# Reordering the first loads, centring before the first transposes, moving two transposes to DMA, and splitting the last output tile of a fused attention + gMLP kernel

## The chip, the cores and the metric

The kernel runs on one core of a Trainium2 chip. The metric is device time in microseconds (us) of one execution; lower is better. All executions told of here were fast (granted TensorE clock 0.994 to 1.0). A "profile" or "trace" is one execution recorded by the hardware profiler; its span is about 1.7 us shorter than the time of the same execution.

Engines: PE is TensorE (matmuls), PEld its weight loads, DVE is VectorE, ACT is ScalarE, POOL is GpSimd, SP is SyncE, which only issues DMAs here. A "q" after an engine's name (SPq) means its sequencer.

## The reference, cut to what matters

With S = 2048 tokens, D = 512, 32 heads of 16, a sliding window of 256, and Fh = 688:

```python
xn = layernorm(x)                                   # over D
A  = attention(xn @ wqkv) @ wo                      # causal, window 256
z  = gelu(xn @ w_in)                                # (S, 1376)
z1, z2 = z[:, :688], layernorm(z[:, 688:])
g  = w_sp @ z2 + b_sp[:, None]                      # mixes over tokens
out = x + A + (z1 * g) @ w_out
```

## The kernel before

Tokens are cut into 16 tiles of 128. The program has three stages. First, for each tile: normalise x on VectorE, transpose it (so that D lies on the partitions), and compute z in two halves of 688 columns on TensorE; q, k and v units for blocks of 512 tokens are put between the halves from tile 3 on. Then the last nine q, k, v units and the first scores: the hand-over. Then scores, exponentials, the token mixing g and the output tiles f, interleaved by a list made at build time. These are the parts that the change touches:

```python
# loads, in the order of issue (nc.sync = SyncE, nc.scalar = ScalarE)
load_x(nc.sync, 0, 1)
load_x(nc.scalar, 1, 2)
load_x(nc.sync, 2, 3)
load_x(nc.scalar, 3, 4)
nc.sync.dma_start(out=w_in_sb[:, :, 0:FH], in_=w_in_v[:, :, 0:FH])     # first half of w_in
nc.sync.dma_start(out=w_in_sb[:, :, FH:F], in_=w_in_v[:, :, FH:F])     # second half
load_x(nc.sync, 4, 8)
nc.sync.dma_start(out=wqkv[:], in_=A_wqkv.rearrange("(c p) f -> p c f", p=P))
# ... the rest of x, b_sp, wo, w_out; zero fill of v_bd on POOL, DVE and ACT;
#     13 warm-up matmuls on zeros ...

def ln_apply(n):            # xn = (x - mean) * rstd; rstd is a power taken on GpSimd
    ...
def transposes(n, xn):
    if n >= 8:
        nc.sync.dma_start_transpose(out=xnT[:, :, n * P : (n + 1) * P], in_=xn[:])
        return
    tp = psum["f"].tile([P, NC, P], BF, name="tp", tag="f")
    for c in range(NC):
        nc.tensor.transpose(out=tp[:, c, :], in_=xn[:, c * P : (c + 1) * P], identity=ident[:])
    nc.scalar.copy(out=xnT[:, :, n * P : (n + 1) * P], in_=tp[:])

def z_half(n, half):        # 8 matmuls of 344 columns, then gelu on ScalarE
    zp = ps_s.tile([P, 2, 512], F32, name="zp", tag="S")
    for c in range(NC):
        for j in range(2):
            f0 = half * FH + j * HALF
            nc.tensor.matmul(zp[:, j, 0:HALF], lhsT=xnT[:, c, n * P : (n + 1) * P],
                             rhs=w_in_sb[:, c, f0 : f0 + HALF], ...)
    nc.scalar.activation(out=..., in_=zp[:, :, 0:HALF], func=ACT.Gelu_apprx_tanh)

# start of the main loop over tiles, cut: z_half(0,0), transposes(1), z_half(0,1),
# transposes(2), z_half(1,0), z_half(1,1), transposes(3), ...

# in f_work(t), the output tile: ten matmuls of 512 columns, one addition, one store
nc.vector.tensor_tensor(out=xo[:], in0=fo[:], in1=xo[:], op=ALU.add)
eng.dma_start(out=out2[t * P : (t + 1) * P, :], in_=xo[:])
```

The softmax here doesn't subtract the row's maximum and nothing guards it: scores larger than these inputs give would overflow.

Of the kernel before, what the change touches and what calls it, by code (L numbers as in the profile page):

```python
# [8 lines left out]
P = 128  # L9
# [6 lines left out]
D = 512  # L16
# [21 lines left out]
OBUF = 8  # L38
UBUF = 4

@with_exitstack
def kernel(
# [50 lines left out]
    def qkv_unit(b, i):  # L93
# [22 lines left out]
        else:  # L116
# [11 lines left out]
            for e in range(2):  # L128
                for kk in range(2):
                    nc.sync.dma_start(  # L130
                        out=v_bd[e * KB : (e + 1) * KB, v_at(2 * n + kk, e), :, :],
                        in_=st[kk * KB : (kk + 1) * KB, e, :, :],
                    )
# [9 lines left out]

    qkv_list = [(b, i) for b in range(4) for i in (0, 1, 8, 2, 3, 9, 4, 5, 10, 11, 6, 7)]

# [8 lines left out]
    with ExitStack() as actx:  # L154
# [11 lines left out]

        w_in_v = B_w_in.rearrange("(c p) f -> p c f", p=P)
        load_x(nc.sync, 0, 1)
        load_x(nc.scalar, 1, 2)
        load_x(nc.sync, 2, 3)  # L170
        load_x(nc.scalar, 3, 4)
        nc.sync.dma_start(out=w_in_sb[:, :, 0:FH], in_=w_in_v[:, :, 0:FH])
        nc.sync.dma_start(out=w_in_sb[:, :, FH:F], in_=w_in_v[:, :, FH:F])
        load_x(nc.sync, 4, 8)
        nc.sync.dma_start(out=wqkv[:], in_=A_wqkv.rearrange("(c p) f -> p c f", p=P))
        load_x(nc.sync, 8, 12)
        load_x(nc.sync, 12, 16)
        with nc.allow_non_contiguous_dma(reason="tiny bias gather"):
            nc.sync.dma_start(out=b_bf[:], in_=B_b_sp.rearrange("(n p) -> p n", p=P))
        nc.sync.dma_start(out=wo_sb[:], in_=A_wo.rearrange("(c p) n -> p c n", p=P))  # L180
        nc.sync.dma_start(
            out=w_out_sb[:, 0:5, :], in_=B_w_out[0:640, :].rearrange("(c p) n -> p c n", p=P)
        )
        nc.vector.memset(w_out_sb[:, 5, :], 0.0)
        nc.sync.dma_start(out=w_out_sb[0:48, 5, :], in_=B_w_out[640:688, :])

# [3 lines left out]
        nc.vector.memset(warm[:], 0.0)  # L190
        wz = lt.tile([P, P], BF, name="wz", bufs=1)
        nc.vector.memset(wz[:], 0.0)
        nc.gpsimd.memset(v_f[:, 0:2560], 0.0)
        nc.vector.memset(v_f[:, 2560:4608], 0.0)
        wps = psum["o"].tile([P, 512], F32, name="wps", tag="o")
        for _ in range(13):
            nc.tensor.matmul(
                wps[:], lhsT=wz[:], rhs=wz[:].unsqueeze(1).to_broadcast([P, 4, P]),
                start=True, stop=True,
            )  # L200
        nc.scalar.activation(out=warm[:, 0:4], in_=warm[:, 4:8], func=ACT.Gelu_apprx_tanh)
        zsrc = warm[:, 4:5].to_broadcast([P, VZ - 4608])
        nc.scalar.copy(out=v_f[:, 4608:VZ], in_=zsrc)
        make_identity(nc, ident[:])
        def setup_early():
            nc.vector.reduce_sum(
                out=hmask[:],
                in_=ident[:].rearrange("p (s e d) -> p e s d", s=4, e=2),
                axis=mybir.AxisListType.XY,
            )  # L210
            for e in range(2):
                nc.vector.memset(v_bd[e * KB : (e + 1) * KB, NKB, :, e : e + 1], 1.0)

        def setup_late():
# [36 lines left out]
        def ln_batch(b0, k):  # L251
            mvt = sm.tile([P, 4, 2], F32, name="mvt")
            for n in range(b0, b0 + k):
# [5 lines left out]
                yield  # L259

        def ln_apply(n):
            xs = xts[n // 4][:, n % 4, :]
            xn = lt.tile([P, D], BF, name="xn")
            nc.vector.tensor_scalar(
                out=xn[:], in0=xs, scalar1=mvx[n], scalar2=rsx[n],
                op0=ALU.subtract, op1=ALU.mult,
            )
            return xn

        def transposes(n, xn):  # L270
            if n >= 8:
                nc.sync.dma_start_transpose(out=xnT[:, :, n * P : (n + 1) * P], in_=xn[:])
                return
            tp = psum["f"].tile([P, NC, P], BF, name="tp", tag="f")
            for c in range(NC):
                nc.tensor.transpose(  # L276
                    out=tp[:, c, :], in_=xn[:, c * P : (c + 1) * P], identity=ident[:]
                )
            nc.scalar.copy(out=xnT[:, :, n * P : (n + 1) * P], in_=tp[:])

        def z_half(n, half):
            zp = ps_s.tile([P, 2, 512], F32, name="zp", tag="S")
            for c in range(NC):
                for j in range(2):
                    f0 = half * FH + j * HALF
                    nc.tensor.matmul(  # L286
                        zp[:, j, 0:HALF],
                        lhsT=xnT[:, c, n * P : (n + 1) * P],
                        rhs=w_in_sb[:, c, f0 : f0 + HALF],
                        start=(c == 0), stop=(c == NC - 1),  # L290
                    )
            dst = (z1 if half == 0 else z2n)[:, n, :]
            nc.scalar.activation(  # L293
                out=dst.rearrange("p (j f) -> p j f", j=2),
                in_=zp[:, :, 0:HALF], func=ACT.Gelu_apprx_tanh,
            )

# [21 lines left out]
        xns = {}  # L319
        for _ in ln_batch(0, 1):  # L320
            pass
        for _ in ln_batch(1, 1):
            pass
        xns[0] = ln_apply(0)
        for _ in ln_batch(2, 1):
            pass
        xns[1] = ln_apply(1)
        for _ in ln_batch(3, 1):
            pass
        for n in range(2, 4):  # L330
            xns[n] = ln_apply(n)
        transposes(0, xns.pop(0))

        z_rs = {}
        for n in range(NB):
            b, j = divmod(n, 4)
            z_half(n, 0)
            if n == 0:
                transposes(1, xns.pop(1))
            elif n == 6:  # L340
                setup_late()
            elif n in (9, 10):
                load_wsp(n - 9)
            if b < 3:
                if j < 2:
                    for _ in ln_batch(4 * b + 4 + 2 * j, 2):
                        pass
                if 1 <= j < 3:
                    for m in range(2):
                        k = 4 * b + 4 + 2 * (j - 1) + m  # L350
                        xns[k] = ln_apply(k)
                        if k >= 8:
                            transposes(k, xns.pop(k))
            if n >= 1:
                r = z_stats(n - 1)
                if r is not None:
                    z_rs[n - 1] = r
            if n >= 3:
                for _ in qkv_unit(*qkv_list.pop(0)):
                    pass  # L360
            z_half(n, 1)
            if n == 0:
                transposes(2, xns.pop(2))
            elif n == 1:
                transposes(3, xns.pop(3))
                setup_early()
# [4 lines left out]
            if n >= 3:  # L371
                for _ in range(2):
                    for _ in qkv_unit(*qkv_list.pop(0)):
                        pass
            if b == 0 and j >= 2:
                for m in range(2):
                    k = 4 + 2 * (j - 2) + m
                    transposes(k, xns.pop(k))
        nc.scalar.activation(out=warm[:, 0:4], in_=warm[:, 4:8], func=ACT.Exp)
# [36 lines left out]
    def e_tile(u):  # L416
        i = u % NE
        if i not in E_sb:
            E_sb[i] = Et = (ep if i < 2 else late()).tile([P, EW], BF, name=f"E{i}", bufs=1)
            nc.vector.memset(  # L420
                Et[:, 0 : 8 * (REG + KB)].rearrange("p (r c) -> p r c", c=REG + KB)[:, :, 0:KB],
                0.0,
            )
            nc.vector.memset(Et[:, 4 * ROW : TOFF], 0.0)
        return E_sb[i]

    for u in range(2):
# [61 lines left out]
    def f_work(t):  # L489
# [4 lines left out]
        xo = xos.pop(t)  # L494
        fo = ps_x.tile([P, 512], F32, name="fo", tag="f")
        for ch in range(NFC):
            nc.tensor.matmul(  # L497
                fo[:], lhsT=uTs[t][:, ch, :], rhs=w_out_sb[:, ch, :],
                start=(ch == 0), stop=False,
            )  # L500
            yield 512 / 2400.0
        for c in range(NC):
            nc.tensor.matmul(  # L503
                fo[:], lhsT=oTs[t][:, c, :], rhs=wo_sb[:, c, :],
                start=False, stop=(c == NC - 1),
            )
            yield 512 / 2400.0
        nc.vector.tensor_tensor(out=xo[:], in0=fo[:], in1=xo[:], op=ALU.add)  # L508
        eng = nc.sync if t >= NB - 2 else nc.gpsimd
        eng.dma_start(out=out2[t * P : (t + 1) * P, :], in_=xo[:])  # L510
        yield -on_dve(0.7)
# [113 lines left out]
    def do_mask(u, kind):  # L625
        Et = e_tile(u)
        mAC, mCA = mACA[:, 0:2, :], mACA[:, 1:3, :]
        if kind == "T":
# [120 lines left out]
```

## Time and profile before

Six executions took 273.22 to 275.02 us, median 273.87.

| Reading | Value | View |
|---|---|---|
| TensorE busy | 264.4 of 272.3 us | the page, part 1 |
| waits of TensorE for data | 4.3 us, all before 11 us | the wait table |
| TensorE idle from 18 to 80 us, and from 80 to 268 us | 0 and about 0.2 us | the table of stretches |
| first half of w_in lands, second half lands | 8.36, 10.59 us | the trace |
| last matmul to end of span | 3.4 us | timeline |

The head of the page of the kernel before, with busy time and share of the span for each engine:

```profile
span 272.3 us, 8364 instructions
PE 264.4 (97%) x3565; PEld 160.5 (59%) x3565; DVE 153.8 (56%) x421; ACT 198.3 (73%) x269; POOL 35.7 (13%) x80
```

The wait table of TensorE in the kernel before (total us, times, longest us):

```profile
PE zp L286 <- DMA w_in_sb<-in_B_w_in_dram: 2.7, 2, 2.0
PE wps L197 <- DVE wz L192: 1.4, 1, 1.4
PE tp L276 <- DVE xn L264: 0.2, 1, 0.2
```

Two stretches of the kernel before (stretch, its length, then busy us of PE, PEld, DVE, ACT and POOL with counts, the granted clock, the DMA share and GB/s):

```profile
18.00:80.00 62.00, 62.00 (x361) 34.77 (x360) 41.86 (x123) 38.42 (x60) 10.00 (x20) 1.00 0.38 80
95.00:240.00 145.00, 144.90 (x2847) 94.28 (x2847) 82.31 (x221) 137.06 (x177) 13.85 (x34) 1.00 0.52 96
```

TensorE sets the pace from 11 us to the last matmul. ScalarE is nearly as full from 95 to 240 us (137.06 of 145 us), but nothing shows TensorE waiting for it. So what can be won lies at the two ends. The timeline of TensorE at the start of the kernel before (start us, us, engine, line, operation, output and inputs, shape, count, and in brackets the idle time before it and who ended it):

```profile
6.01 0.40 PE L276 MATMUL tp<-ident,xn 128*128 128x128 bf16 x4 [0.23 <-DVE xn L264]
8.40 1.33 PE L286 MATMUL zp<-w_in_sb,xnT 128*128 128x344 bf16 x8 [2.00 <-DMA w_in_sb<-in_B_w_in_dram]
9.57 0.39 PE L276 MATMUL tp<-ident,xn 128*128 128x128 bf16 x4
10.63 1.33 PE L286 MATMUL zp<-w_in_sb,xnT 128*128 128x344 bf16 x8 [0.68 <-DMA w_in_sb<-in_B_w_in_dram]
11.80 0.39 PE L276 MATMUL tp<-ident,xn 128*128 128x128 bf16 x4
```

After 10.63 us there is no gap. TensorE has then one z half and one transpose group behind it (1.17 + 0.23 us by their starts), so the stream runs as if it had begun at 9.23 us. And the end, the last VectorE addition of the kernel before:

```profile
268.95 0.69 DVE L508 TENSOR_TENSOR xo<-fo,xo 128x512 bf16<-128x512 f32 x1 [1.47 <-PE fo L503]
```

### The profile page before, as it was taken

The numbers are of one execution on the slowest core, as the hardware profiler recorded it, in microseconds if no ns is written. First come the engines' busy times: TensorE is split into PE (matmuls) and PEld (weight loads), VectorE is DVE, ScalarE is ACT, GpSimd is POOL, SyncE is SP. The second block draws the span as 40 slices with busy tenths as digits, with TensorE's granted clock in tenths as the row PEclk, the third lists the DMA queues.
The fourth block names the chain that finished last, engine by engine and source line by source line (L and its number), as shares of the span: only waits on it lengthen the run. The fifth ranks groups of instructions, "written<-read, shape, count | busy, mean of one in ns | idle before, by whom it ended". The sixth has DMA issues, their size and how long they took to land.

```text
span 272.3 us, 8364 instructions
## 1 busy us (share of the span) xinstructions
PE 264.4 (97%) x3565; PEld 160.5 (59%) x3565; DVE 153.8 (56%) x421; ACT 198.3 (73%) x269; POOL 35.7 (13%) x80
## 2 busy tenths in 40 slices
PE   7699999999999999999999999999999999999995
PEld 2465555555554566667675666757575666766652
DVE  7597965954637465645645655565556466522222
ACT  7477556555567889999999999999999999200000
POOL 6122412111101001010101010101010101101110
PEclk9999999999999999999999999999999999999999
DMA  6975141375211248452709273637161446456621
GB/s 208 376 185 181 40 78 39 83 94 120 45 30 24 50 62 171 94 141 42 147 3 173 48 116 74 113 25 162 31 158 37 112 61 128 90 126 144 144 70 59
DMA packets 73078, 27.84 MB, mean 102 GB/s; under 512 B 62944, under 2 KB 71568, under 8 KB 73040
## 3 DMA queue, kind: packets, MB, share of 16 engines
q1 hardware_dynamic: 71312, 23.10, 41.9%
q0 software_dynamic: 1440, 3.93, 4.9%
q8 instruction: 28, 0.46, 0.7%
q10 hardware_dynamic: 288, 0.26, 0.3%
q14 instruction: 10, 0.08, 0.1%
HBM read 8.41 MB, written 2.10 MB: 39 GB/s over the span
## 4 chain that ended last, share of the span: by engine, by line
PE 90%; DMA 4%; DVE 2%; ACT 1%; SPq 1%; issue 0%; POOL 0%; DVEq 0%; ACTq 0%; POOLq 0%
PE gf L469 27%; PE o L540 14%; PE zp L286 13%; PE S L593 9%; PE fo L497 8%; PE fo L503 5%; PE pj_f L100 4%; PE pj_o L100 4%; DMA w_in_sb<-in_B_w_in_dram 3%; PE pj_f L119 2%; PE pj_o L119 2%; ACT E L614 1%; DMA v_bd<-vst 1%; PE tp L276 0%; SPq L130 0%; ACT kst L109 0%
## 5 line engine op out<-in xcount | busy, mean ns | idle before, releaser
L614 ACT ACTIVATE E<-S 128x1024 bf16<-128x1024 f32 (+3 forms) x184 | 141.5, 893 | 1.2 <-DMA v_bd<-vst 0.7
L469 PE MATMUL gf<-z2n,wspT 128*128 128x344 bf16 x512 | 85.0, 310 | 0.0
L469 PEld LDWEIGHTS <-wspT 128*128 128x128 bf16 x512 | 45.9, 97 | 25.5 <-issue 2.6
L620 DVE TENSOR_TENSOR E<-E,mACA 128x1024 bf16<-128x1024 bf16 (+1 forms) x92 | 42.4, 500 | 11.6 <-ACT E L614 11.1
L540 PEld LDWEIGHTS <-E 128*128 128x128 bf16 x1440 | 41.7, 96 | 6.9 <-issue 2.4
L540 PE MATMUL o<-v_bd,E 128*128 128x48 bf16 x1440 | 45.0, 183 | 0.0
L286 PE MATMUL zp<-w_in_sb,xnT 128*128 128x344 bf16 x256 | 42.2, 309 | 2.7 <-DMA w_in_sb<-in_B_w_in_dram 2.7
L475 DVE SCALAR_TENSOR_TENSOR u<-gf,b_all,z 128x344 bf16<-128x344 f32 x32 | 18.4, 575 | 38.3 <-PE gf L469 31.0
L286 PEld LDWEIGHTS <-xnT 128*128 128x128 bf16 x256 | 24.8, 98 | 18.0 <-issue 2.0
L593 PE MATMUL S<-qT,kpad 32*128 32x192 bf16 (+3 forms) x960 | 30.4, 231 | 0.1
L510 POOL DMA_DIRECT2D out_dram<-xo x14 | 7.6, 545 | 146.7 <-DVE xo L508 146.7
L497 PE MATMUL fo<-w_out_sb,uT 128*128 128x512 bf16 x96 | 24.4, 379 | 0.0
L593 PEld LDWEIGHTS <-kpad 32*128 32x128 bf16 x960 | 14.0, 92 | 17.5 <-issue 16.6
L508 DVE TENSOR_TENSOR xo<-fo,xo 128x512 bf16<-128x512 f32 x16 | 11.1, 691 | 22.1 <-PE fo L503 22.1
L111 DVE TENSOR_SCALAR kpad<-kst,hmask 128x512 bf16<-128x512 bf16 x32 | 9.8, 349 | 22.1 <-ACT kst L109 22.0
L246 POOL TENSOR_TENSOR rs<-ve,mhalf 128x2 f32<-128x2 f32 (+1 forms) x18 | 12.4, 687 | 66.1 <-DVE ve L243 66.1
L293 ACT ACTIVATE z<-zp 128x688 bf16<-128x688 f32 x16 | 11.9, 743 | 11.8 <-PE zp L286 11.8
L293 ACT ACTIVATE z2n<-zp 128x688 bf16<-128x688 f32 x16 | 11.9, 743 | 11.5 <-PE zp L286 11.5
L100 PEld LDWEIGHTS <-wqkv 128*128 128x128 bf16 x128 | 12.5, 98 | 11.9
L503 PE MATMUL fo<-wo_sb,oT 128*128 128x512 bf16 x64 | 17.3, 380 | 0.0
L100 PE MATMUL pj_o<-xnT,wqkv 128*128 128x512 bf16 x64 | 16.4, 379 | 0.0
L100 PE MATMUL pj_f<-xnT,wqkv 128*128 128x512 bf16 x64 | 16.4, 379 | 0.0
(54 smaller groups left out, 179.7 us busy)
## 6 DMA issues: line engine op xcount, KB each, us to landing
v_bd<-vst SPq DMA_DIRECT2D x64, 32.0 KB, 1.9
xo<-in_A_x_dram POOLq DMA_DIRECT2D x16, 128.0 KB, 3.4
out_dram<-xo POOLq DMA_DIRECT2D x14, 128.0 KB, 2.6
xt<-in_A_x_dram SPq DMA_DIRECT2D x3, 512.0 KB, 11.8
wqkv<-in_A_wqkv_dram SPq DMA_DIRECT2D x1, 1536.0 KB, 12.7
w_in_sb<-in_B_w_in_dram SPq DMA_DIRECT2D x2, 688.0 KB, 7.5
w_out_sb<-in_B_w_out_dram SPq DMA_DIRECT2D x1, 640.0 KB, 5.9
wo_sb<-in_A_wo_dram SPq DMA_DIRECT2D x1, 512.0 KB, 11.7
```

Source lines behind the costliest of these rows:

```text
L100: nc.tensor.matmul(pt[:], lhsT=wqkv[:, c, w0 : w0 + P], rhs=xnT[:, c, t0 : t0 + 512], start=(c == 0), stop=(c == NC - 1),)
L246: nc.gpsimd.tensor_tensor(out=rs[:, 0:k], in0=ve[:, 0:k], in1=mhalf[:, 0:k], op=ALU.pow)
L286: nc.tensor.matmul(zp[:, j, 0:HALF], lhsT=xnT[:, c, n * P : (n + 1) * P], rhs=w_in_sb[:, c, f0 : f0 + HALF], start=(c == 0), stop=(c == NC ...
L293: nc.scalar.activation(out=dst.rearrange("p (j f) -> p j f", j=2), in_=zp[:, :, 0:HALF], func=ACT.Gelu_apprx_tanh,)
L469: nc.tensor.matmul(gf[:, 0:HALF], lhsT=wspT[t][:, c, :], rhs=z2n[:, c, j * HALF : (j + 1) * HALF], start=(c == 0), stop=(c == NB - 1),)
L475: nc.vector.scalar_tensor_tensor(out=u[:, j * HALF : (j + 1) * HALF], in0=gf[:, 0:HALF], scalar=b_all[:, t : t + 1], in1=z1[:, t, j * HALF ...
L497: nc.tensor.matmul(fo[:], lhsT=uTs[t][:, ch, :], rhs=w_out_sb[:, ch, :], start=(ch == 0), stop=False,)
L503: nc.tensor.matmul(fo[:], lhsT=oTs[t][:, c, :], rhs=wo_sb[:, c, :], start=False, stop=(c == NC - 1),)
L540: nc.tensor.matmul(o[:, q, s, :], lhsT=Et[:, col : col + P], rhs=v_bd[:, v_at(kb, 0) : v_at(kb, 1) + 1 : kb + 1, 4 * G + s, :], start=(i = ...
L593: nc.tensor.matmul(S[s // 2][:, s % 2, col : col + n * KB], lhsT=kpad[32 * s : 32 * s + 32, G, kb, :, :].rearrange("p e k -> p (e k)"), rh ...
L614: nc.scalar.activation(out=dst, in_=src, func=ACT.Exp, scale=SM_SCALE)
L620: nc.vector.tensor_tensor(out=ap, in0=ap, in1=m.unsqueeze(1).to_broadcast([P, ap.shape[1], 2, KB]), op=ALU.mult,)
```

## The change

The intent is to give TensorE useful work earlier, take a little work off it, and shorten the end. In short:

1. Loads: x blocks 2 and 3 go behind the first half of w_in; its second half comes as two quarters; all from SyncE; the later loads are held back.
2. Tiles 0 and 1 are centred (mean subtracted) and transposed at once on TensorE; 1/std goes into the scale of the gelu. For q, k and v they are also normalised and transposed by DMA.
3. The z half (0,1) is done in two quarters, with tile 1's first half between them.
4. Tiles 6 and 7 are transposed by DMA, not on TensorE.
5. Hand-over: another order of the last q, k, v units, half of the last v transfers from GpSimd, gap memsets of the exponentials' buffers later.
6. The last output tile is done in 320 + 192 columns.
7. Smaller things at the start: the warm-up is cut into 8 + 6 matmuls (13 before), a part of ScalarE's zero fill goes to GpSimd, and the transposed copies of tiles 1 and 2 are made by VectorE.

```diff
         load_x(nc.sync, 0, 1)
-        load_x(nc.scalar, 1, 2)
+        load_x(nc.sync, 1, 2)
+        load_w(0, FH)
         load_x(nc.sync, 2, 3)
-        load_x(nc.scalar, 3, 4)
-        nc.sync.dma_start(out=w_in_sb[:, :, 0:FH], in_=w_in_v[:, :, 0:FH])
-        nc.sync.dma_start(out=w_in_sb[:, :, FH:F], in_=w_in_v[:, :, FH:F])
+        load_w(FH, FH + HALF)
+        load_x(nc.sync, 3, 4)
+        load_w(FH + HALF, F)
         load_x(nc.sync, 4, 8)
-        nc.sync.dma_start(out=wqkv[:], in_=A_wqkv.rearrange("(c p) f -> p c f", p=P))
+        (q and k thirds of wqkv here; v third and x 8..15 in load_more(), after the first tiles;
+         b_sp, wo, w_out in load_late(), at tile 7)
...
-        for _ in range(13):          (warm-up matmuls)
+        warm_up(8)                   (six more after the first transposes)
...
+        def ln_center(n):
+            xc = lt.tile([P, D], BF, name="xn")
+            nc.vector.tensor_scalar(out=xc[:], in0=xts[n // 4][:, n % 4, :], scalar1=mvx[n],
+                                    scalar2=None, op0=ALU.subtract)
+            return xc
-        def transposes(n, xn):
-            if n >= 8:
+        def transposes(n, xn, centered=False):
+            if not centered and (n < 2 or n >= DMA_T):       (DMA_T = 6)
                 nc.sync.dma_start_transpose(out=xnT[:, :, n * P : (n + 1) * P], in_=xn[:])
...
+            if n == 0:
+                xc1 = ln_stats_center(1)
+                ln_only(2)
+                z_half(0, 0)
+                transposes(1, xc1, True)
+                transposes(0, ln_apply(0))
+                xns[2] = ln_apply(2)
+                transposes(1, ln_apply(1))
+                load_more()
+                z_half(0, 1, (0,))
+                continue
             z_half(n, 0)
+            if n == 1:
+                transposes(2, xns.pop(2)); ln_only(3); xns[3] = ln_apply(3)
+                z_half(0, 1, (1,))
...
-        fo = ps_x.tile([P, 512], F32, name="fo", tag="f")       (ten matmuls, addition, store)
+        parts = [(0, D)] if t < NB - 1 else [(0, 320), (320, D)]
+        for a, b in parts:                                      (the same on columns a:b)
```

## The prediction

> **What bounds the kernel now.** TensorE. The page gives it 264.4 us busy of a 272.3 us span; the wait table has only 4.3 us of waits, all before 11 us; in the table of stretches TensorE idles 0.2 us in all between 18 and 268 us. ScalarE is nearly full from 95 to 238 us, but TensorE shows no wait for it. So only an earlier start of useful TensorE work, less of it, or a shorter tail can help. Of 7.9 us idle, some 4.5 are at the start and 3.4 after the last matmul (268.9 us).
>
> **Start.** The chain of waits begins with w_in's transfer: its first half lands at 8.4 us, its second at 10.6; only from 10.63 us does TensorE run without a gap. By then it had done one z half (1.17 us in the chain) and one transpose group (0.23), so the stream behaves as if begun at 9.2 us. The change puts x blocks 2 and 3 (256 KB) behind the first w_in half and splits the second into two quarters with 688-byte rows; z_half(0,1) is split to match. In 0.5 us slices, the DMA engines move 250 to 340 GB/s from 2.5 us on, so 256 KB less in front is about 0.8 us: first half at about 7.6 us. The centred transpose takes the GpSimd power (0.57 us) off the way of x block 0; its xcT should be ready near 6 us, before the weights, so by itself it buys nothing. The next quarter lands at about 9.1 to 9.5 us; TensorE wants it at 9.0. I allow 0.2 to 0.5 us of stalls. The Trainium skill, "DMA: Bandwidth & Descriptors", Specifications, puts the line-rate minimum at 512 B, so 688 B should be no disaster; no run here shows that yet. Net: 1.3 us (0.5 to 1.7).
>
> **Work removed.** Tiles 6 and 7 are transposed by DMA: two groups of about 0.22 us, 0.45 us. Tiles 0 and 1 get both a TensorE transpose (centred) and a DMA transpose for q, k, v. Those queue behind 3.5 MB of loads and are needed near 16.5 us; I expect them at 15 to 16 us. This is the thinnest margin.
>
> **Hand-over (80 to 98 us).** With v transfers earlier and on two queues and gap memsets later, VectorE's 1.8 us wait for v_bd and ScalarE's 0.7 us go away, but TensorE idled only about 0.2 us there. Gain 0.1 us.
>
> **Tail.** The last tile is split 320+192. The last VectorE addition falls from 0.69 to about 0.36 us (estimate by columns plus a fixed part); ten more short matmuls add some 0.05; the last store (1.7 us to landing) is mostly fixed cost. Gain 0.3 us.
>
> **Sum:** 1.3 + 0.45 + 0.1 + 0.3 = 2.1 us of 273.87: predicted 271.7 us, range 270.5 to 273.1. Faster by over 2%: 0.02; within 2%: 0.96; slower by over 2%: 0.02.
>
> **Right or wrong would show as:** first z matmul at about 7.6 us (before: 8.40) and gapless TensorE from about 11.5 us with more work done; 24 transposing matmuls instead of 32; VectorE's wait for v_bd gone while TensorE's idle there hardly changes; the end 3.1 us after the last matmul instead of 3.4.
>
> **What would make it wrong:** quarters moving slower than halves; DMA transposes of tiles 0 and 1 landing after 16.5 us, which stalls the first q unit; TensorE's clock falling back in the new warm-up; ScalarE pacing the middle, so that an earlier start is swallowed there.

## The result, and the profile after

The changed kernel took 270.43 to 270.97 us in eight runs, median 270.82; the kernel before, 273.72 us (median of 16). The ratio is 0.9889, with a 95% interval of 0.9873 to 0.9905. A ratio here is the mean time of one kernel's fast runs over that of the other's in the same rounds, so it is not quite the ratio of the medians. The gain is 2.9 us, 1.1%: inside the range of the prediction, but only 0.3 us from its lower end, and 0.8 us more than forecast. The spread also shrank, from 2.1 us (272.9 to 275.02) to 0.5 us.

The head of the page of the changed kernel, and its wait table of TensorE:

```profile
span 269.0 us, 8406 instructions
PE 264.3 (98%) x3568; PEld 160.7 (60%) x3568; DVE 155.3 (58%) x426; ACT 197.0 (73%) x267; POOL 40.3 (15%) x88
```

```profile
PE wps L204 <- DVE wz L191: 1.1, 1, 1.1
PE zp L342 <- DMA w_in_sb<-in_B_w_in_dram: 0.5, 1, 0.5
PE gf L556 <- DVE on L641: 0.3, 1, 0.3
```

TensorE is busy as long as before; what went is idle time. The wait for w_in fell from 2.7 to 0.5 us; one new wait of 0.3 us appeared in the hand-over. The timeline of TensorE at the start of the changed kernel:

```profile
4.66 0.42 PE L311 MATMUL tp<-ident,xn 128*128 128x128 bf16 x4
4.92 1.46 PE L204 MATMUL wps<-wz 128*128 128x512 bf16 x6
6.91 1.33 PE L342 MATMUL zp<-w_in_sb,xcT 128*128 128x344 bf16 x8 [0.53 <-DMA w_in_sb<-in_B_w_in_dram]
8.07 0.39 PE L311 MATMUL tp<-ident,xn 128*128 128x128 bf16 x4
8.42 0.74 PE L324 MATMUL zo<-w_in_sb,xcT 128*128 128x344 bf16 x4
9.00 1.33 PE L342 MATMUL zp<-w_in_sb,xcT 128*128 128x344 bf16 x8
```

From 6.91 us on it runs almost without a gap: the quarter at 8.42 us costs about 0.1 us. The last additions of the changed kernel, one for each part of the last tile:

```profile
265.40 0.49 DVE L597 TENSOR_TENSOR xo<-fo,xo 128x320 bf16<-128x320 f32 x1 [0.67 <-PE fo L592]
266.22 0.36 DVE L597 TENSOR_TENSOR xo<-fo,xo 128x192 bf16<-128x192 f32 x1 [0.33 <-PE fo L592]
```

To see where the time came from, I read four marks of TensorE's stream in each trace (starts in us; the fourth is the end of the last matmul):

```
               first z   first q,k,v   first score   last matmul ends   span
before           8.40       18.52         89.95          268.91         272.3
after            6.91       15.96         87.22          266.19         269.0
gained           1.49        2.56          2.73            2.72           3.3
```

The lines behind the marks, from the timelines of TensorE, first in the kernel before and then in the changed one (first q, k, v unit, first score, last matmuls):

```profile
18.52 1.03 PE L100 MATMUL pj_o<-xnT,wqkv 128*128 128x512 bf16 x4
89.95 0.37 PE L593 MATMUL S<-qT,kpad 32*128 32x192 bf16 x8
267.88 1.03 PE L503 MATMUL fo<-wo_sb,oT 128*128 128x512 bf16 x4
```

```profile
15.96 1.03 PE L101 MATMUL pj_o<-xnT,wqkv 128*128 128x512 bf16 x4
87.22 0.37 PE L682 MATMUL S<-qT,kpad 32*128 32x192 bf16 x8
265.69 0.49 PE L592 MATMUL fo<-wo_sb,oT 128*128 128x192 bf16 x4
```

(These two profiled executions lie 3.3 us apart; the medians 2.9.) The 2.56 us before the first q, k, v unit hold the 0.45 us of two transpose groups: the kernel before has done tiles 4 and 5 by then, the changed one does them just after, and later has no groups for 6 and 7. So the start gave 2.1 us, the transposes 0.45, the hand-over 0.16, the stage from the first score to the last matmul nothing, and the tail 0.55.

The trace also tells when each of the 16 shares of a DMA (one for each DMA engine) reported its landing. Here for the first half of w_in:

```
                 first   9th      12th   last share      second half, last share
before            5.82    6.55    6.74     8.36               10.59
after             5.68    6.03    6.18     6.87                9.80
```

The fastest share gained 0.14 us and the slowest 1.49. TensorE waits for the slowest. The 9th of the 16 came 0.52 us earlier; the rest of the 1.49 is that the last two shares no longer come 1.6 us behind the 12th. That was not foreseen, and most experiments below ask for its cause.

### The profile page after: what moved, and what is told of

It is laid out like the page before. It is cut to its first block, busy times and chain, and to the rows that moved or that the text cites. A ratio compares the mean times of both kernels' runs of the same rounds, so it can differ in the third digit from the quotient of the medians.

```text
span 269.0 us, 8406 instructions
## 1 busy us (share of the span) xinstructions
PE 264.3 (98%) x3568; PEld 160.7 (60%) x3568; DVE 155.3 (58%) x426; ACT 197.0 (73%) x267; POOL 40.3 (15%) x88
## 4 chain that ended last, share of the span: by engine, by line
PE 96%; DMA 2%; DVE 1%; SPq 0%; issue 0%; DVEq 0%
PE gf L556 29%; PE o L629 14%; PE zp L342 14%; PE S L682 9%; PE fo L586 8%; PE pj_o L101 6%; PE fo L592 5%; PE pj_f L101 5%; PE pj_f L120 3%; PE pj_o L120 2%; DMA w_in_sb<-in_B_w_in_dram 2%; PE zo L324 0%; PE tp L311 0%; SPq L164 0%; DVE u L562 0%
## 5 line engine op out<-in xcount | busy, mean ns | idle before, releaser
L342 PE MATMUL zp<-w_in_sb,xnT 128*128 128x344 bf16 x224 | 37.2, 309 | 0.0
L342 PEld LDWEIGHTS <-xnT 128*128 128x128 bf16 x224 | 21.7, 98 | 14.1 <-ACT xnT L315 0.3
L586 PE MATMUL fo<-w_out_sb,uT 128*128 128x512 bf16 (+2 forms) x102 | 24.5, 367 | 0.0
L597 DVE TENSOR_TENSOR xo<-fo,xo 128x512 bf16<-128x512 f32 (+2 forms) x17 | 11.2, 660 | 21.6 <-PE fo L592 21.6
L101 PE MATMUL pj_o<-xnT,wqkv 128*128 128x512 bf16 x72 | 18.5, 379 | 0.0
L351 ACT ACTIVATE z<-zp 128x688 bf16<-128x688 f32 x14 | 10.4, 743 | 10.2 <-PE zp L342 10.2
L592 PE MATMUL fo<-wo_sb,oT 128*128 128x512 bf16 (+2 forms) x68 | 17.5, 368 | 0.0
L351 ACT ACTIVATE z2n<-zp 128x688 bf16<-128x688 f32 x14 | 10.4, 743 | 9.3 <-PE zp L342 9.3
L641 DVE TENSOR_TENSOR on<-o,rsum 128x128 bf16<-128x128 f32 x64 | 15.6, 286 | 1.4 <-DVE rsum L639 0.3
```

What stands on the lines that cost most here:

```text
L101: nc.tensor.matmul(pt[:], lhsT=wqkv[:, c, w0 : w0 + P], rhs=xnT[:, c, t0 : t0 + 512], start=(c == 0), stop=(c == NC - 1),)
L342: nc.tensor.matmul(zp[:, j, 0:HALF], lhsT=xcT[n][:, c, :] if n in xcT else xnT[:, c, n * P : (n + 1) * P], rhs=w_in_sb[:, c, f0 : f0 + HAL ...
L351: nc.scalar.activation(out=dst.rearrange("p (j f) -> p j f", j=2), in_=zp[:, :, 0:HALF], func=ACT.Gelu_apprx_tanh, scale=rsx[n] if n in xc ...
L586: nc.tensor.matmul(fo[:, a:b], lhsT=uTs[t][:, ch, :], rhs=w_out_sb[:, ch, a:b], start=(ch == 0), stop=False,)
L592: nc.tensor.matmul(fo[:, a:b], lhsT=oTs[t][:, c, :], rhs=wo_sb[:, c, a:b], start=False, stop=(c == NC - 1),)
L641: nc.vector.tensor_tensor(out=o_norm[J][q][:, G * P : (G + 1) * P].rearrange("p (s e d) -> p s e d", e=2, d=DH), in0=o[:, q, :, :].rearran ...
```

## The experiments

Each kernel was run against the kernel before on the same chip. "Changed kernel + edit" starts from the changed one. The intervals on the ratios are 0.2 to 0.4% each way, mostly from the spread of the kernel before; where a few tenths of a microsecond matter I lean on the marks in the traces. "Worse than the changed kernel" compares medians taken in different rounds and on different chips. By the ratios the losses would be 0.6 us (a_xfirst), 0.3 (a_twoqueues), 0.7 (a_zorder), 0.2 (a_handover), 0.4 (a_whole), 2.4 (a_nocentre) and 1.8 (a_t8tail), so a few tenths either way are not settled.

### Which part of the load order brings the weights earlier?

**b_onequeue**: the kernel before, all x loads from SyncE.

```diff
-        load_x(nc.scalar, 1, 2)
+        load_x(nc.sync, 1, 2)
-        load_x(nc.scalar, 3, 4)
+        load_x(nc.sync, 3, 4)
```

> The kernel before, with x blocks 1 and 3 issued from SyncE like the others, same order of loads (x0, x1, x2, x3, first half of w_in). Before: first w_in half landed at 8.36 us, 12 of its 16 engine shares by 6.74, the last two 1.6 us later; after: last at 6.87, 12th at 6.18. Order theory (only the 256 KB in front matter): landing 8.4 us or later, time as before. Queue theory (the second issuing queue leaves a few DMA engines behind): spread between 12th and last share under 0.8 us, landing about 7.6 us, time 0.7 us better. Fill theory (ScalarE's zero fill of v_bd, which ran to 6.4 us before and 4.9 us after, slows the transfer): fill ends about 0.9 us earlier, landing some 0.4 us better.

Measured: 273.40 us, ratio 0.9992 (0.9967 to 1.0018). First half landed at 8.52 us, 12th share at 7.43. The queue theory falls as it was put: nothing came earlier and the time stayed. The test is not clean, though. With four x loads on one engine w_in is issued 0.94 us later (2.67 against 1.73 us), and from issue to landing it took 5.85 us instead of 6.63. The unchanged time agrees with the Trainium skill, "DMA: Bandwidth & Descriptors", section "Issuing engines are not separate DMA queues": issuing from several engines saves only sequencer time.

**b_latefill**: the kernel before, without ScalarE's zero fill of v_bd at the start.

```diff
-        zsrc = warm[:, 4:5].to_broadcast([P, VZ - 4608])
-        nc.scalar.copy(out=v_f[:, 4608:VZ], in_=zsrc)
...
                 transposes(3, xns.pop(3))
+                nc.gpsimd.memset(v_f[:, 4608:VZ], 0.0)
```

> The kernel before, with ScalarE's share of the zero fill moved to GpSimd after the first tiles; loads and both queues unchanged. Order theory and queue theory: first w_in half still at 8.4 us with its last two shares 1.6 us behind, time as before. Fill theory: landing at about 7.6 us or earlier, spread gone, time 0.7 us better or more.

Measured: 273.74 us, ratio 1.0008 (0.999 to 1.0027). First half landed at 8.23 us. The fill theory falls: the last shares no longer trailed (12th at 7.88 us), but the landing and the time stayed.

**a_xfirst**: changed kernel, x blocks 2 and 3 in front of w_in again.

```diff
+        load_x(nc.sync, 2, 3)
+        load_x(nc.sync, 3, 4)
         load_w(0, FH)
-        load_x(nc.sync, 2, 3)
         load_w(FH, FH + HALF)
-        load_x(nc.sync, 3, 4)
         load_w(FH + HALF, F)
```

> The changed kernel with x blocks 2 and 3 put back in front of the first w_in half (all on one queue). All theories: the landing moves from 6.87 to about 7.6 us (256 KB at 340 GB/s). If order were the whole of the 1.5 us, it should go back to 8.4 us. Time 0.5 to 0.8 us worse than the changed kernel (about 271.5).

Measured: 271.06 us, 0.24 us worse than the changed kernel's median; ratio to before 0.9911 (0.9893 to 0.9929). First half landed at 7.22 us, not 8.4; that is 0.35 us later than in the profile of the changed kernel, and 0.8 to 0.9 later than in a_handover and a_t8tail, which have its loads. The order is a small part of the gain: its undoing costs 0.24 us of 2.9 by the medians, 0.6 by the ratios.

**a_twoqueues**: changed kernel, x block 1 from ScalarE.

```diff
-        load_x(nc.sync, 1, 2)
+        load_x(nc.scalar, 1, 2)
```

> The changed kernel with x block 1 alone issued from ScalarE (second queue). Order theory: landing stays at 6.9 us, time as the changed kernel (270.8). Queue theory: shares spread again by over 1.2 us, landing 7.6 us or later, time 0.5 us worse or more. Fill theory: fill starts 0.45 us later, landing at most 0.3 us later.

Measured: 270.86 us, as the changed kernel. Here the shares did spread (12th at 5.49, last at 7.06 us), and yet the time stayed: w_in was issued 0.47 us earlier, so its slowest share was no later than in the profile of the changed kernel by more than 0.2 us (but by 0.6 to 0.8 us than in five other kernels built on the changed one, 6.28 to 6.47 us). So a second queue may well widen the spread; it is not what cost the time here.

Over all twelve experiments and the two kernels, the landing of the first half sorts by family: 8.23 to 8.52 us in the four kernels built on the one before, 6.28 to 7.22 in the ones built on the changed kernel that load it in one piece, whichever part was undone. The kernels that share their loads exactly with the changed one and start alike landed it at 6.28, 6.40 and 6.87 us, so one profile is good to about 0.6 us. What separates the families by a further microsecond is neither the order alone, nor the second queue alone, nor the zero fill alone, nor (a_whole, below) the size of the piece behind it; combinations were not run. The plainest pair is b_onequeue and a_xfirst: in both, SyncE loads x blocks 0 to 3 and then the first half of w_in, issued at 2.67 us, and it landed at 8.52 and at 7.22 us. **It stays open.** The DMA packets tell where the time went, not why: in the four kernels built on the one before, 34 to 71 of the 1024 packets of 1376 bytes took over 1.6 times the usual 59 ns, the last of these as late as 7.7 to 9.9 us; in a_whole, which loads the same two pieces, 37 did, the last at 6.7 us. The one large part of the load change that no run undid by itself is the holding back of the later loads (the rest of x, the v weights, b_sp, wo, w_out, and wqkv in thirds); that is a suspect, not a finding. Against it speaks that a_chunks and a_chunks2 (below), which hold back still more, again have late slow packets: 25 and 22 of their 1024 packets of 688 bytes, up to 8.0 and 9.6 us, where the changed kernel has none.

### What does TensorE do while it waits?

**a_zorder**: changed kernel, z half (0,1) done whole before tile 1.

```diff
                 z_half(0, 1, (0,))
+                z_half(0, 1, (1,))
                 continue
...
                 xns[3] = ln_apply(3)
-                z_half(0, 1, (1,))
```

> The changed kernel with the second z half of tile 0 done whole, right after its first quarter, before tile 1 (loads unchanged). What-TensorE-does-while-it-waits theory: the last quarter lands at about 9.8 us, TensorE reaches it at about 9.05 us, idles 0.7 to 0.9 us, and has less work behind it: time 0.5 to 0.9 us worse than the changed kernel (about 271.5). Load-order theory (the gain is all in the earlier first half): no change beyond 0.2 us.

Measured: 271.44 us, 0.6 worse than the changed kernel; ratio to before 0.9914. The size came as expected, the cause only in part. From first z to first q, k, v unit it took 9.46 us, against 9.05 in the changed kernel; but the last quarter landed at 9.25 us, so TensorE lost only about 0.17 us there (two matmuls start 0.32 us apart instead of 0.15). The larger part shows 5 us later, where VectorE's chain for tile 3 now starts after a later transpose of tile 2, and TensorE waits 0.27 us. The other 0.24 us of this trace came ahead of the first z, as these lines of the timeline of a_zorder show:

```profile
5.07 2.25 PE L204 MATMUL wps<-wz 128*128 128x512 bf16 x6
7.15 1.33 PE L342 MATMUL zp<-w_in_sb,xcT 128*128 128x344 bf16 x8
14.04 0.40 PE L311 MATMUL tp<-ident,xn 128*128 128x128 bf16 x4 [0.27 <-DVE xn L291]
```

The weights were there at 6.30 us, but TensorE was still at the six warm-up matmuls (wps), which took 2.25 us here and 1.46 in the changed kernel's profile. The edit does not touch them, so this part is chance of the execution. TensorE works in order here: filler in front of real work delays it (z 0.85 us after its weights). The Trainium skill, "TensorE: Matmul & The Clock Gate", Part 1, says that the array runs at half rate until it has been busy through a window of about 3.4 us, and that these windows do not start with the kernel. The traces agree in kind: the first eight warm-up matmuls of the changed kernel took 3.59 us, about 0.43 us each by their starts, and later ones of the same size 0.22; when the change falls differs from execution to execution (after seven slow matmuls in the kernel before, after none of the thirteen in b_zorder). The granted-clock row shows 1.0 throughout and does not tell of it.

**b_zorder**: the kernel before, tile 1's first half ahead of tile 0's second half.

```diff
             z_half(n, 0)
+            if n == 1:
+                z_half(0, 1)
...
-            z_half(n, 1)
+            if n > 0:
+                z_half(n, 1)
```

> The kernel before with only the order of z halves changed: tile 1's first half ahead of tile 0's second half; loads as before. What-TensorE-does-while-it-waits theory: one more z half (1.17 us) fits before the second w_in half lands at about 10.5 us, less 0.6 us for the wait on tile 1's transposed copy: 0.6 to 1.2 us better than before (ratio about 0.997). Load-order theory: no change.

Measured: 274.20 us, ratio 1.0013 (0.9987 to 1.0039): no gain. The timeline of b_zorder, TensorE and then ScalarE, says why:

```profile
8.33 1.33 PE L286 MATMUL zp<-w_in_sb,xnT 128*128 128x344 bf16 x8 [1.02 <-DMA w_in_sb<-in_B_w_in_dram]
9.50 0.61 PE L276 MATMUL tp<-ident,xn 128*128 128x128 bf16 x8
10.97 3.67 PE L286 MATMUL zp<-w_in_sb,xnT 128*128 128x344 bf16 x24 [0.87 <-ACT xnT L279]
```

```profile
9.70 0.74 ACT L293 ACTIVATE z<-zp 128x688 bf16<-128x688 f32 x1 [1.76 <-PE zp L286]
10.34 1.07 ACT L279 COPY xnT<-tp 128x512 bf16<-128x512 bf16 x2
```

Tile 1's transposed copy waits behind the gelu of tile 0 on ScalarE, and is ready only at 10.9 us, when the second half of w_in (10.42 us) is there too. The order alone is worth nothing; in the changed kernel tile 1's copy lies on VectorE, and there the order pays (a_zorder: about 0.4 us in the trace).

**a_whole**: changed kernel, second half of w_in in one piece.

```diff
-        load_w(FH, FH + HALF)
-        load_x(nc.sync, 3, 4)
-        load_w(FH + HALF, F)
+        load_w(FH, F)
+        load_x(nc.sync, 3, 4)
```

> The changed kernel with the second w_in half loaded in one piece instead of two quarters (x block 3 behind it). TensorE reaches its first use at about 7.9 to 8.4 us, and the whole lands at 9.3 to 9.8: idle 1.2 to 1.6 us, time 0.8 to 1.4 us worse than the changed kernel (271.6 to 272.2). Also tells whether what follows in the queue matters for the first half: if the big piece behind it is why the kernels before land it at 8.2 to 8.5 us, it lands here later than 7.5 us; else at 6.3 to 6.9.

Measured: 271.00 us; ratio to before 0.9905 (0.9864 to 0.9945). The wait that the quarters take away is there, from the wait table of a_whole:

```profile
PE zo L323 <- DMA w_in_sb<-in_B_w_in_dram: 0.7, 1, 0.7
```

It is half of what I expected, since the whole piece landed at 8.70 us. From first z to first q, k, v unit: 9.78 us against 9.05, so the split is worth 0.7 us in the trace, but 0.2 us by the medians, which were taken in different rounds (0.4 by the ratios). The first half landed at 6.45 us: the big piece behind it does not slow it.

**a_nocentre**: changed kernel without centring (normalise first, transpose once).

```diff
-        transposes(0, ln_stats_center(0), True)
+        ln_only(0)
+        transposes(0, ln_apply(0))
...
-                xc1 = ln_stats_center(1)
+                ln_only(1)
+                xc1 = ln_apply(1)
                 ln_only(2)
                 z_half(0, 0)
-                transposes(1, xc1, True)
-                transposes(0, ln_apply(0))
+                transposes(1, xc1)
                 xns[2] = ln_apply(2)
-                transposes(1, ln_apply(1))
```

> The changed kernel without the centred transposes: tiles 0 and 1 are normalised first and transposed once, on TensorE, and the two DMA transposes fall away. The prediction said that centring buys nothing by itself, as the weights come later: then the first z matmul stays at 6.3 to 6.9 us and the time within 0.3 us of the changed kernel (270.8). Rival (x block 0 sets the start): first z matmul 0.6 to 0.9 us later and the time as much worse. Tile 1 may add up to 0.4 us, since its power on GpSimd now stands in its way.

Measured: 271.57 us in the profiled execution, but 273.15, 273.46 and 273.78 in the three timed ones (median 273.31, ratio 0.9978). The trace of the profiled one:

```profile
5.57 0.40 PE L311 MATMUL tp<-ident,xn 128*128 128x128 bf16 x4 [1.22 <-DVE xn L291]
5.81 1.46 PE L204 MATMUL wps<-wz 128*128 128x512 bf16 x6
7.10 1.33 PE L342 MATMUL zp<-w_in_sb,xnT 128*128 128x344 bf16 x8
```

The weights were there at 6.47 us. The transpose comes 0.9 us later than in the changed kernel, and the warm-up matmuls behind it with it, so z starts at 7.10 us, 0.6 after the weights. So centring buys a good half microsecond here, most of it by way of the warm-up: the copy of the transposed tile ended at 6.54 us, only 0.07 after the weights, and the filler behind the later transpose did the rest. Of the 0.85 us between the two profiled executions 0.66 lies after the last matmul, where a late store has nothing to do with centring (1.95 us to landing instead of 1.51). The three timed executions lost 2.3 to 3.0 us, nearly the whole gain. No trace of one of them exists, so this stays open; in the profiled one, matmuls already ran at 0.22 us each right after TensorE's gap of 1.22 us, so it shows no loss of clock.

### The hand-over, the two transposes and the tail

**a_handover**: changed kernel, part 5 undone.

```diff
-                    (nc.gpsimd if b == 3 and e else nc.sync).dma_start(
+                    nc.sync.dma_start(
...
-    qkv_list = [(b, i) for b in range(3) for i in (0, 1, 8, 2, 3, 9, 4, 5, 10, 11, 6, 7)]
-    qkv_list += [(3, i) for i in (0, 8, 1, 9, 2, 10, 3, 11, 4, 5, 6, 7)]
+    qkv_list = [(b, i) for b in range(4) for i in (0, 1, 8, 2, 3, 9, 4, 5, 10, 11, 6, 7)]
...                     (gap memsets again when a buffer is first taken)
```

> The changed kernel with the hand-over part undone (order of the last q, k, v units, the GpSimd share of v transfers, the time of the gap memsets). The trace shows the gain at the first score matmul (2.72 us) equal to that at the last matmul (2.73), so: no change, within 0.2 us of the changed kernel, although VectorE's wait of about 1.8 us for v_bd should come back. A rival (the hand-over is worth 0.5 us or more): 271.3 or more.

Measured: 270.93 us, as the changed kernel; ratio 0.9895 (0.9868 to 0.9921). The timeline of VectorE in the kernel before, and then in a_handover, has the same wait:

```profile
96.25 0.27 DVE L420 MEMSET E<- 128x256 uint32 x1 [1.82 <-DMA v_bd<-vst]
```

```profile
93.38 0.27 DVE L507 MEMSET E<- 128x256 uint32 x1 [1.87 <-DMA v_bd<-vst]
```

In the changed kernel it is gone, and that is worth next to nothing: from first q, k, v unit to first score it took 71.43 us with part 5 undone and 71.26 with it, a difference of 0.17 us (0.35 up to the last matmul). VectorE was not what TensorE waited for.

**a_t8tail**: changed kernel, parts 4 and 6 undone, which lie far apart in time.

```diff
-DMA_T = 6
+DMA_T = 8
...
-        parts = [(0, D)] if t < NB - 1 else [(0, 320), (320, D)]
+        parts = [(0, D)]
```

> The changed kernel with two separate parts undone: tiles 6 and 7 transposed on TensorE again (32 transposing matmuls in all), and the last tile's output in one part. The stream to the last matmul should be 0.45 us longer, and the time from the last matmul to the end 3.4 instead of 2.8 us: together 1.0 us worse (271.8). Prediction's own sizes for the two: 0.45 and 0.3, together 0.75 (271.6).

Measured: 272.37 us; ratio to before 0.9955 (0.9919 to 0.9991), 1.5 us worse than the changed kernel. In the trace, first q, k, v unit to the start of the last z matmul took 62.47 us, against 61.41: 1.06 us for two transpose groups. A part of that is this wait, from the timeline of a_t8tail:

```profile
21.72 0.39 PE L311 MATMUL tp<-ident,xn 128*128 128x128 bf16 x4
22.55 0.38 PE L311 MATMUL tp<-ident,xn 128*128 128x128 bf16 x4 [0.45 <-ACT qT L107]
```

The second group waits until ScalarE has made its copy of q (qT), which has the PSUM buffer that comes free next. In the kernel before no such wait showed, so against it the DMA transposes are worth 0.45 us, but in the changed program taking them away would cost twice that. From the last matmul to the end: 3.6 us against 2.8; of these 0.8, 0.33 are the shorter addition (0.36 us, not 0.69) 0.27 the store (1.51 us from issue to landing for 48 KB, 1.78 for 128 KB), and the rest comes after the landing. In the kernel before that end took 3.4 us. (The two parts add up to more than the loss of the execution, as the first z of a_t8tail came 0.47 us earlier.)

### Two attempts at a faster version

**a_chunks**: first half of w_in in four pieces along the contraction, so that the first z half could start on the first piece; tile 1 transposed before it, its copy on ScalarE; both first halves ahead of the quarters; the k weights behind the DMA transposes.

```diff
-        load_w(0, FH)
+        for c in range(NC):
+            load_w(0, FH, c, c + 1)
         load_x(nc.sync, 2, 3)
         load_w(FH, FH + HALF)
-        load_x(nc.sync, 3, 4)
         load_w(FH + HALF, F)
+        load_x(nc.sync, 3, 4)
...
-                xc1 = ln_stats_center(1)
-                ln_only(2)
+                transposes(1, ln_stats_center(1), True)
                 z_half(0, 0)
-                transposes(1, xc1, True)
+                z_half(1, 0)
+                z_half(0, 1, (0,))
...
-                z_half(0, 1, (0,))
+                z_half(1, 1, (0,))
```

> A version meant to beat both: the first w_in half loaded in four pieces along the contraction, tile 1 transposed before the first z half, both first halves done before the second half's quarters are needed, k weights loaded behind the two DMA transposes. Expected: TensorE starts z at 6.0 to 6.5 us on the first piece, ends it about 0.3 us after the last piece lands, and 0.5 to 1.3 us better than the changed kernel (269.5 to 270.3). If the start is bounded by something other than the first half's landing, no gain; if the DMA transposes of tiles 0 and 1 come late, a wait before the first q unit at about 14.7 us.

Measured: 272.30 us, 1.5 worse than the changed kernel (ratio to before 0.9943). The wait table of a_chunks:

```profile
PE tp L312 <- DVE xn L292: 1.5, 1, 1.5
```

VectorE could not write tile 3's xn: in its timeline that instruction waited 1.87 us for the DMA transpose of tile 0 to free a buffer:

```profile
14.12 0.41 DVE L292 TENSOR_SCALAR xn<-xt,mvt,rs 128x512 bf16<-128x512 bf16 x1 [1.87 <-DMA xnT<-xn]
```

Since the pieces landed from 4.58 us on (the last at 6.82) and z began only at 6.90, behind warm-up and tile 1's transposes, the early pieces were not used either.

**a_chunks2** mends both: centred tiles in space not yet used, x block 3 earlier, two warm-up matmuls after the first transposes.

```diff
-            xc = lt.tile([P, D], BF, name="xn")
+            xc = z2n[:, NB - 1 - n, 0:D]
-        warm_up(6)
+        warm_up(2)
...     (x block 3 before the last quarter; its statistics one step earlier; copies on ScalarE)
```

> Second attempt at a version that beats both. The first (a_chunks) had its z work of tiles 0 and 1 on TensorE about as early as the changed kernel, but idled 1.5 us before tile 3's transposes: VectorE waited for a buffer that the late DMA transpose of tile 0 held, and x block 3 came later. Here the centred tiles lie in space not yet used, so no buffer waits; x block 3 goes before the last quarter; two warm-up matmul groups instead of six. Expected: first z matmul at 5.9 to 6.3 us, tile 3's transposes at about 12.2 us, no wait above 0.3 us after 7 us: 0.6 to 1.3 us better than the changed kernel (269.5 to 270.2). If the weights' landing alone sets the pace, no gain beyond 0.3 us.

Measured: 271.40 us (270.70 to 271.57), ratio to before 0.9915: 0.6 worse than the changed kernel. z began at 6.16 us, 0.75 earlier, but the last of the four pieces landed at 7.17 and the last quarter at 10.67 us (9.80 in the changed kernel). The wait table of a_chunks2 has the wait on that quarter:

```profile
PE zo L325 <- DMA w_in_sb<-in_B_w_in_dram: 0.3, 1, 0.3
```

The first q, k, v unit came at 15.70 us, within the changed kernel's own scatter (15.48 to 15.96 in three executions with the same start). Starting earlier on the first piece moved the wait to the last. In this trace the whole loss lies later: from first score to last matmul it took 179.69 us instead of 178.97, with a wait of 0.5 us for a late DMA transpose of u that the changed kernel does not show, and from there to the end 3.16 instead of 2.83. One trace cannot tell whether that is chance. No version beat the changed kernel.

## Why the prediction was right or wrong

- **Bound by TensorE, gain only at the ends: right.** From first score to last matmul the two kernels differ by 0.01 us. ScalarE swallowed nothing.
- **Start, 1.3 us predicted, 2.1 measured: the step that was mis-sized.** Two terms of it were off. "First half at about 7.6 us": it landed at 6.87 in the profile of the changed kernel, and at 6.28 and 6.40 in two kernels with the same start. Dividing 256 KB by the rate was about right for the order: with x blocks 2 and 3 back in front (a_xfirst) it landed at 7.22 us. What the prediction did not have is the further microsecond up to the 8.23 to 8.52 us of the kernels built on the one before. A transfer is finished when its slowest share is, and the shares lay up to 2.5 us apart before (5.82 to 8.36) and 1.2 after; why, the runs do not show. That the total stayed within the range although this was missing owes something to luck. "0.2 to 0.5 us of stalls" for the quarters: about 0.1 us (the first quarter took 0.70 in the chain where the second took 0.58).
- **"By itself it buys nothing" (centring): wrong.** That judged it against weights at 7.6 us. With weights at 6.3 to 6.9 us the longer path of x block 0 and the warm-up behind it set the start (a_nocentre: first z 0.6 us after the weights landed, and 2.3 to 3.0 us lost in the timed executions, for a reason that is open).
- **The 688-byte rows: right.** In the trace of the changed kernel a packet of 688 bytes took 34 ns in the median, one of 1376 bytes 59 ns: 20 against 23 bytes per ns. The Trainium skill, "DMA: Bandwidth & Descriptors", Specifications, names 512 B as the minimum for line rate; the trace agrees that 688 is no cliff.
- **DMA transposes of tiles 0 and 1: right, with a thin margin.** They landed at 14.90 and 15.36 us; the first q unit began at 15.96 without a wait.
- **Work removed, 0.45 us: right** against the kernel before. Undoing it in the changed program costs 1.06 us, as a new wait comes with it.
- **Hand-over, 0.1 us: right.** 0.16 by the marks, 0.17 by undoing it (0.35 up to the last matmul, 0.1 by the medians). VectorE's 1.8 us went away and TensorE did not notice.
- **Tail, 0.3 us predicted, 0.55 measured: the other mis-sized term.** The addition was right (0.36 us). "The last store is mostly fixed cost" was too coarse: it landed in 1.51 us, not 1.71. The same page of the skill ("Anatomy of one DMA") fits a DMA issued from GpSimd as about 2.0 us + bytes / 436e3; its slope gives an estimate of 0.19 us for 80 KB less, which is the 0.20 measured, while its fixed part is larger than what these SyncE stores show.

The runs isolate no single carrier of the gain. By the medians, undoing the load order costs 0.2 us, the quarters 0.2 (0.7 in the trace), the order of z halves 0.6 (0.4 of it in the trace), the transposes and the tail together 1.5. Undoing the centring costs 2.5, nearly the whole gain, of which the one trace explains about 0.6. Doing the z order alone in the kernel before gives nothing, so at least this part of the start needs others.

## What to carry to other kernels

When one engine is full from end to end, look at its first gapless instruction and its last one, and count what it has done by then; here, work on other engines in the middle was free, and so was their waiting. Expect a load to end with its slowest share: read all the shares' landings before dividing bytes by a rate, and judge each part of a change against the others' new times, not the old ones. On an engine that works in order, filler and evacuations stand in the way of what is behind them: b_zorder lost its point to a gelu placed ahead of a copy, and in a_zorder and a_nocentre warm-up matmuls kept z waiting.

## What the Trainium skill lacked or had wrong

- "DMA: Bandwidth & Descriptors" tells that up to 16 engines each report their share, but has no figure for how far apart the shares of one load land: 1.2 us (changed kernel) to 2.5 us (before) for 688 KB, and the lag stays on the loads behind it (second half: 7.91 to 10.59 us).
- No page tells how uneven packets of one size are at the start of a kernel: of the 512 packets of 1376 bytes in the changed kernel, 36 took over 1.6 times the usual 59 ns (247 ns in the median), all from 2.9 to 4.7 us; in the kernel before 57 of 1024 did, the last at 9.2 us. They came with the first packets of the tensor in the one trace and not only there in the other; the cause is not shown.
- The fit in the same page ("Anatomy of one DMA", about 2.0 us + bytes / 436e3) is for DMAs issued from GpSimd, and the page gives none for SyncE. The last stores from SyncE here took 1.51 us (48 KB; 1.95 once, in a_nocentre), 1.6 (80 KB) and 1.71 to 1.78 (128 KB): the slope holds, the fixed part is about 1.4 us. The last store of 128 KB from GpSimd took 1.98 us, where the fit gives 2.3.
- "TensorE: Matmul & The Clock Gate" is right that the moment of full rate varies (after seven slow warm-up matmuls in the kernel before, eleven in b_onequeue), but does not say that the granted-clock row of such a profile stays at 1.0 meanwhile (all slices here), nor what an in-order warm-up can cost: in a_zorder z began 0.85 us after its weights landed.
